# A transformer block's front on one core: unit products ahead of the first products, two chunks turned by TensorE, the first raw tile in halves, another order of loads

## Chip, cores, metric

The kernel runs on one core of a Trainium2 chip. The metric is the device time of one execution in microseconds, median of several. All values in this document are from executions of the fast state. A ratio of times is between executions of the same rounds on the same chip; the parts read from traces are compared across chips, since nearly every kernel was traced on one chip only.

## The reference

The inputs are q, k, v of 8 x 8 x 576 x 64, a norm gain, two weight matrices of 512 x 2048 and 2048 x 512, and two scalars.

```python
kv  = einsum('bhsd,bhse->bhde', k, v)
out = einsum('bhsd,bhde->bhse', q, kv)
x   = out / sqrt(mean(out*out, -1) + 1e-6) * g_norm      # -> (4608, 512)
h   = x @ w_in
y   = (s * relu(h)**2 + b) @ w_out                       # float32
```

## The kernel before

Tokens are handled in chunks of 128 rows; chunks 0 to 3 form the first block and are the only ones computed ahead of the first dense product. The weights come in as raw tiles `w_raw` of 128 x 1024 words, are converted by ScalarE (high words, low words) and put together by VectorE (a shift, an add). "Turned" means transposed; "Square" is ScalarE's pass over an attention product that begins its norm, and "root" the square root in it. The dense products ("slots", 16 records in the trace each: a float32 product makes two records, a transpose one; in after the first 18 unit products are 36 records, the four transposes of a q chunk 4) need converted weights `wa`, `wb` and the turned, normed rows `xT`. All that follows concerns the first 40 us. `x6(1)` below is the dense product whose weights are `w_t`; b_ps is the small product that spreads the bias.

```python
def kv_product(b):
    for i in range(2):                      # the two halves of k and v
        kv = kv_in.pop((b, i))
        ...                                 # 36 products of 64x64
    ...                                     # copies to bd_kv: ScalarE l=0, VectorE l=1

def attention(c, first=False):
    def turn():                             # q chunk -> qT
        for p in range(NP):
            nc.tensor.transpose(ps[:, p, :], q_in[c][:, p * P : p * P + P], ident)
        if first: nc.vector.tensor_copy(out=st["qT"], in_=ps)
        else:     nc.scalar.copy(st["qT"], ps)
    def product():                          # 16 products of 32 rows, then the sum of squares
        ...
        nc.scalar.activation(st["xn"], st["x"], AF.Square)
        nc.vector.reduce_sum(st["ss"], st["xn"], axis=mybir.AxisListType.X)
    def norm(): ...                         # root on ScalarE, inverse and product on VectorE
    def turn_x():                           # VectorE turns, ScalarE scales 128x256, 4 times for 2 chunks
        nc.vector.transpose(out=to, in_=...)
        ...

# the front
load_q(0, two); send_w(); load_q(2)
for _ in range(2): send_w()
kv_product(0)
turn[0](); turn[1](); product[0](); product[1](); norm[0]()
hi(0); turn[2](); norm[1](); shift(0); turn_x[0](); lo(0); plus(0)
product[2](); turn[3](); turn_x[1](); product[3]()
hi(1); norm[2](); shift(1); lo(1); plus(1); norm[3]()
slots0[0](); turn_x[2](); turn_x[3]()
for step in (hi, lo, shift, plus): step(2)
slots0[1]()
```

`hi` and `lo` are ScalarE's conversions of a raw tile, `shift` and `plus` are VectorE's two steps.

Of the kernel before, what the change touches and what calls it, by code (L numbers as in the profile page):

```python
# [8 lines left out]
FP32 = mybir.dt.float32  # L9
U32 = mybir.dt.uint32  # L10
# [5 lines left out]
def kernel(  # L16
# [96 lines left out]
    def load_q(c, queues=(nc.sync, nc.sync)):  # L113



        t = qp.tile([P, 2 * DM], FP32, name="q_sb", tag="q")
        pieces = []
        for i in range(2):
            if c + i < R:  # L120
                q_in[c + i] = t[:, i * DM : i * DM + DM]
                to = q_in[c + i].rearrange("p (h d) -> p h d", h=H)
                for s, (b, j, _) in enumerate(parts(c + i)):
                    queues[s].dma_start(
                        out=to[s * HB : s * HB + HB],
                        in_=q[b].rearrange("h (p j) d -> p j h d", j=R)[:, j],
                    )
                continue
            w = 4 * i
            for b, j, n in parts(c + i):  # L130
                if pieces and pieces[-1][1] == b and pieces[-1][2] + pieces[-1][3] == j:
                    pieces[-1][3] += n
                else:
                    pieces.append([w, b, j, n])
                w += n
            q_in[c + i] = t.rearrange("p (a w) -> p a w", a=NP)[:, :, i * P : i * P + P]
            if c + i == R:
                q_in[R] = t[:, DM:].rearrange("p (a w) -> p a w", a=NP)
        for w, b, j, n in pieces:
            src = q[b].rearrange("h (t j) d -> h t j d", j=JC)  # L140
            to = t.rearrange("p (a w d) -> p a w d", a=NP, d=32)
            if c < R:
                to, w = t[:, DM:].rearrange("p (a w d) -> p a w d", a=NP, d=32), 0
            for h in range(H):
                for a in range(2):
                    rows = slice(32 * (2 * (h % 2) + a), 32 * (2 * (h % 2) + a) + 32)
                    nc.sync.dma_start(
                        out=to[rows, h // 2, w : w + n, :],
                        in_=src[h, :, j : j + n, a * 32 : a * 32 + 32],
                    )  # L150
# [32 lines left out]



    def pairs(i):
        return w_raw[i].rearrange("p (n two) -> p n two", two=2)

    def fold_hi(i):
        if wide:  # L190
            hi = w_raw[i].bitcast(FP32).rearrange("p (n two) -> p n two", two=2)[:, :, 1]
            nc.scalar.activation(hi, hi, AF.Prelu, scale=2.0**-112, alpha=-(2.0**32))

    def round_lo(i):
        if wide:
            lo = pairs(i)[:, :, 0]
            nc.scalar.activation(lo, lo, AF.Copy, scale=2.0**-29)

    def shift_hi(i, dst):
        if wide:  # L200
            nc.vector.tensor_scalar(
                out=dst.bitcast(U32), in0=pairs(i)[:, :, 1],
                scalar1=3, scalar2=None, op0=ALU.logical_shift_left,
            )
        else:
            nc.vector.tensor_copy(out=dst, in_=w_raw[i])

    def add_lo(i, dst):
        if wide:
            d = dst.bitcast(U32)  # L210
            nc.vector.tensor_tensor(out=d, in0=d, in1=pairs(i)[:, :, 0], op=ALU.add)
        del w_raw[i]

    def add(o, a, b):
        nc.vector.tensor_tensor(out=o, in0=a, in1=b, op=ALU.add)  # L215
# [92 lines left out]
    nc.gpsimd.dma_start(out=b_col, in_=moe_b.to_broadcast((P, 1)))  # L308
    b_sq = const.tile([P, P], FP32, name="b_sq")
    nc.vector.memset(b_sq, 1.0)  # L310
    nc.vector.tensor_scalar(out=b_sq, in0=b_sq, scalar1=b_col, scalar2=None, op0=ALU.mult)
    b_row = const.tile([P, DM], FP32, name="b_row")

    def bias_row():

        ps = ps_t.tile([P, DM], FP32, name="b_ps", tag="t")
        matmul(ps, b_sq, b_row, True, True)
        nc.scalar.copy(b_row, ps)


    def kv_product(b):


        ps = [ps_t.tile([P, 2, D], FP32, name="kv_ps", tag="t") for _ in range(2)]
        for i in range(2):
            kv = kv_in.pop((b, i))
            for j in range(R):
                for l in range(2):
                    for r in range(2):
                        rows = slice(r * HB, r * HB + HB)  # L330
                        nc.tensor.matmul(  # L331
                            ps[r][l * HB : l * HB + HB, i, :],
                            lhsT=kv[rows, 0, l, j, :],
                            rhs=kv[rows, 1, l, j, :],
                            start=(j == 0),
                            stop=(j == R - 1),
                        )
        for r in range(2):
            for l in range(2):
                ls = slice(l * HB, l * HB + HB)  # L340
                to = bd_kv[b % 2][ls, 2 * r : 2 * r + 2, ls].rearrange("p i (c e) -> p i c e", c=KC)
                src = ps[r][ls].rearrange("p i (e c) -> p i c e", c=KC)
                if b == 0 and l == 1:
                    nc.vector.tensor_copy(out=to, in_=src)
                else:
                    nc.scalar.copy(to, src)
# [3 lines left out]
    def attention(c, first=False):  # L350
# [2 lines left out]



        b, b1 = parts(c)[0][0], parts(c)[-1][0]
        st = {}

        def turn():
            st["qT"] = attp.tile([P, NP, P], FP32, name="qT", tag="qT")  # L360
            if c >= R:
                nc.vector.transpose(out=st["qT"], in_=q_in[c])
                return
            if c == 0:
                ps = ps_a.tile([P, NP, P], FP32, name="qT_ps", tag="x")
            else:
                ps = ps_t.tile([P, NP, P], FP32, name="qT_ps", tag="t")
            for p in range(NP):
                nc.tensor.transpose(ps[:, p, :], q_in[c][:, p * P : p * P + P], ident)  # L369
            if first:  # L370
                nc.vector.tensor_copy(out=st["qT"], in_=ps)
            else:
                nc.scalar.copy(st["qT"], ps)

        def product():
            if first:
                ps = bank_of("att", "xy"[c % 2]).rearrange("p b (m n) -> p (b m) n", m=2)
            else:
                ps = ps_a.tile([P, NP, P], FP32, name="x_ps", tag="x")
            for w in range(4):  # L380
                for p in range(NP):
                    nc.tensor.matmul(  # L382
                        ps[32 * p : 32 * p + 32, w, :],
                        lhsT=st["qT"][:, p, 32 * w : 32 * w + 32],
                        rhs=bd_kv[(b if w < 2 else b1) % 2][:, p, :],
                        start=True,
                        stop=True,
                    )
# [21 lines left out]
        def turn_x():  # L410
            u, j = divmod(c, 4)
            if j == 0:
                xT[u] = xp.tile([P, KC, 2 * TB], FP32, name="xT", tag="xT")
            to = xT[u][:, :, j * P : j * P + P]
            nc.vector.transpose(
                out=to, in_=st["xn"].rearrange("p h d -> p (h d)").rearrange("p (c x) -> p c x", c=KC)
            )
# [4 lines left out]
                        to[:, i], to[:, i], AF.Copy, scale=g_col[:, i : i + 1]  # L422
                    )

        return turn, product, norm, turn_x

    def whole(product, norm):
        def run():
# [54 lines left out]
    def mm1_plain(s):  # L483


        def block(lower, half, name, tag):
            ps = bank_of("c", tag)
            w = (wb if lower else wa)[s]
            for b in range(2):
                for c in range(KC):  # L490
                    matmul(
                        ps[:, b, :], w[:, c, b], xT[0][:, c, half * TB : half * TB + TB],
                        b == 0 and c == 0, c == KC - 1,
                    )
# [269 lines left out]
    def place(n):  # L764
        s, lower = where(n)
        return w_in_at(s, lower) if n < 2 * NS else w_out_at(s, lower)

    def hi(n):
        fold_hi(blocks[n])

    def lo(n):
        round_lo(blocks[n])

    def shift(n):
        shift_hi(blocks[n], place(n))

    def plus(n):
        add_lo(blocks[n], place(n))
        send_w()

    def more(n):

# [9 lines left out]
        load_kv(0, i, kv0p, two, tag="kv")  # L792
    load_q(0, two)
    send_w()
    load_q(2)
    for _ in range(2):
        send_w()
    kv_product(0)
# [1 line left out]
    gp = ctx.enter_context(tc.tile_pool(name="gp", bufs=NS))  # L800


    turn, product, norm, turn_x = zip(*(attention(c, True) for c in range(4)))
    turn[0]()
    turn[1]()
    product[0]()
    product[1]()
    norm[0]()
    hi(0)
    turn[2]()  # L810
    norm[1]()
    shift(0)
    turn_x[0]()
    lo(0)
    plus(0)
    product[2]()
    turn[3]()
    turn_x[1]()
    product[3]()
    hi(1)  # L820
    norm[2]()
    shift(1)
    lo(1)
    plus(1)
    norm[3]()
    slots0 = [slot for s in range(NS) for slot in mm1_plain(s)]
    slots0[0]()
    turn_x[2]()
    turn_x[3]()
    for step in (hi, lo, shift, plus):  # L830
        step(2)
    slots0[1]()

    def side_of(u):

        if u + 1 >= U:
            return {}
        turn, product, norm, turn_x = zip(*(attention(c) for c in range(4 * u + 4, 4 * u + 8)))
        product = [whole(*steps) for steps in zip(product, norm)]
        side = {  # L840
            2: [turn[0]],
# [130 lines left out]
```

## Time and profile before

| | before |
|---|---|
| time, median of 4 | 975.06 us (974.03 to 975.20) |
| span of the profiled execution | 972.7 us |
| TensorE busy | 951.6 us, 98% |
| first slot starts | 27.92 us |
| second slot starts | 33.82 us |
| fourth slot starts | 40.80 us |
| from there to the end | 931.9 us |

The last row is the one to keep: from the fourth slot on TensorE has work all the time, so whatever the front does is seen in the start of the fourth slot, and whatever is given back later is seen in the rest. The rest is "span less start of the fourth slot" throughout.

The prediction shows the main lines. Three more of the timeline of before matter (start in us, length in us, engine, line, operation, tiles, count, and in brackets the idle time of that engine before it with what ended it). They are what VectorE and ScalarE do between the k-v product and the first attention product:

```profile
14.64 0.29 DVE L311 TENSOR_SCALAR b_sq<-b_sq,b_col 128x128 f32<-128x128 f32 x1 [13.61 <-DMA b_col<-in_moe_b_dram]
15.11 0.42 ACT L346 COPY bd_kv<-kv_ps 64x128 f32<-64x128 f32 x2 [13.10 <-PE kv_ps L331]
15.40 0.50 DVE L344 COPY bd_kv<-kv_ps 64x128 f32<-64x128 f32 x2 [0.47 <-ACT bd_kv L346]
```

VectorE stood for 13.61 us at the bias square, since it comes ahead of the copies in its order and its transfer landed at 14.6. Before the change this cost nothing: the k-v product itself ended at 15.0.

### The profile page before, as it was taken

Reading aid. Unit: us, or ns where it says so; the run is one execution under the profiler, and the core shown is the slowest. Engines: PE = TensorE matmul, PEld = TensorE weight load, DVE = VectorE, ACT = ScalarE, POOL = GpSimd, SP = SyncE. Lnnn points to the kernel's source line nnn. Section 1 sums busy time; section 2 is a strip of 40 time slices with the busy share of each in tenths; the row PEclk is TensorE's granted clock in tenths of the full one; section 3 lists DMA queues with packets and bytes.
Section 4 is the critical chain, followed back from the end, with each engine's and each line's share of the span. In section 5 each row is a group of like instructions: output and inputs, shape, how many; then the busy total and the mean of one; then the engine's idle time right before and its main releaser. Section 6 shows DMA issues by size and latency. Waiting matters only on the chain.

```text
span 972.7 us, 15160 instructions
## 1 busy us (share of the span) xinstructions
PE 951.6 (98%) x6406; PEld 824.5 (85%) x6406; DVE 490.1 (50%) x804; ACT 193.4 (20%) x359; POOL 6.7 (1%) x18
## 2 busy tenths in 40 slices
PE   4899999999999999999999999999999999999997
PEld 4788888888888888888888888888888888888886
DVE  2789667454445534554346344644455345544431
ACT  2674132101220112111210212011201111111100
POOL 2000000000000000000000000000000000000000
PEclk9999999999999999999999999999999999999999
DMA  9688828622553346142363256225213440422032
GB/s 237 195 288 254 260 77 213 156 98 97 138 112 111 118 141 136 55 150 67 102 138 147 68 136 154 88 90 149 65 44 130 128 89 16 152 64 117 1 130 86
DMA packets 106931, 121.59 MB, mean 125 GB/s; under 512 B 74352, under 2 KB 80752, under 8 KB 99568
## 3 DMA queue, kind: packets, MB, share of 16 engines
q1 hardware_dynamic: 104816, 119.12, 41.8%
q10 hardware_dynamic: 1728, 1.51, 0.6%
q8 instruction: 50, 0.82, 0.4%
q14 instruction: 17, 0.14, 0.0%
q0 software_dynamic: 320, 0.00, 0.0%
HBM read 103.81 MB, written 16.78 MB: 124 GB/s over the span
## 4 chain that ended last, share of the span: by engine, by line
PE 95%; DMA 2%; DVE 1%; ACT 1%; SPq 0%; issue 0%; ACTq 0%; DVEq 0%
PE x_ps L87 50%; PE y_ps L87 31%; PE z_ps L87 9%; PE x_ps L382 3%; PE kv_ps L331 2%; DMA kv_sb<-in_v_dram 1%; DMA w_sb<-w 1%; PE qT_ps L369 0%; DVE xn L401 0%; ACT xT L421 0%; DVE ss L393 0%; SPq L99 0%; SPq L609 0%; ACT xn L391 0%; DVE o L590 0%
## 5 line engine op out<-in xcount | busy, mean ns | idle before, releaser
L87 PE MATMUL x_ps<-w_sb,a 128*128 128x256 f32 x768 | 172.4, 381 | 0.0
L87 PEld LDWEIGHTS x_ps<-w_sb,a 128*128 128x128 f32 x768 | 144.8, 190 | 21.9 <-issue 2.8
L87 PE MATMUL y_ps<-w_sb,a 128*128 128x256 f32 x640 | 142.9, 380 | 1.3 <-DMA w_sb<-w 1.3
L87 PEld LDWEIGHTS y_ps<-w_sb,a 128*128 128x128 f32 x640 | 120.9, 190 | 19.1 <-DMA w_sb<-w 1.7
L87 PE MATMUL x_ps<-xs,ws 128*128 128x256 f32 x512 | 121.0, 379 | 0.0
L87 PE MATMUL y_ps<-xs,wb 128*128 128x256 f32 x512 | 121.0, 379 | 0.0
L517 ACT COPY r<-x_ps 128x512 f32<-128x512 f32 x96 | 56.3, 586 | 295.7 <-PE x_ps L87 289.0
L87 PEld LDWEIGHTS x_ps<-xs,ws 128*128 128x128 f32 x512 | 97.3, 190 | 13.2
L87 PEld LDWEIGHTS y_ps<-xs,wb 128*128 128x128 f32 x512 | 97.3, 190 | 13.2
L215 DVE TENSOR_TENSOR a<-y_ps,r 128x512 f32<-128x512 f32 x64 | 44.0, 687 | 122.2 <-ACT r L517 122.2
L87 PE MATMUL x_ps<-xT,wa 128*128 128x256 f32 x384 | 91.2, 385 | 0.1
L87 PEld LDWEIGHTS x_ps<-xT,wa 128*128 128x128 f32 x384 | 74.0, 193 | 10.7 <-ACT xT L421 0.3
L474 DVE SCALAR_TENSOR_TENSOR a<-a 128x512 f32<-128x512 f32 x96 | 66.4, 692 | 3.3
L590 DVE SCALAR_TENSOR_TENSOR or<-x_ps,s_col,b_row 128x256 f32<-128x256 f32 x52 | 25.0, 482 | 76.1 <-PE x_ps L87 72.9
L87 PE MATMUL x_ps<-xT,ws 128*128 128x256 f32 x256 | 61.1, 381 | 0.0
L87 PE MATMUL z_ps<-xT,wa 128*128 128x256 f32 x256 | 60.5, 379 | 0.0
L550 DVE TENSOR_TENSOR a<-a 128x512 f32<-128x512 f32 x32 | 22.1, 692 | 76.0 <-ACT a L549 76.0
L391 ACT ACTIVATE xn<-x_ps 128x512 f32<-128x512 f32 x34 | 20.3, 597 | 192.9 <-PE x_ps L382 190.9
L87 PE MATMUL x_ps<-w_sb,s 128*128 128x256 f32 x256 | 57.3, 382 | 0.0
L87 PEld LDWEIGHTS x_ps<-w_sb,s 128*128 128x128 f32 x256 | 48.1, 190 | 7.6 <-issue 1.4
L87 PEld LDWEIGHTS z_ps<-xT,wa 128*128 128x128 f32 x256 | 48.6, 190 | 6.6
L87 PEld LDWEIGHTS x_ps<-xT,ws 128*128 128x128 f32 x256 | 48.1, 190 | 6.7
(94 smaller groups left out, 803.6 us busy)
## 6 DMA issues: line engine op xcount, KB each, us to landing
w_sb<-w SPq DMA_DIRECT2D x56, 1024.0 KB, 5.2
kv_sb<-in_k_dram SPq DMA_DIRECT2D x30, 288.0 KB, 4.8
kv_sb<-in_v_dram SPq DMA_DIRECT2D x30, 288.0 KB, 6.2
w_raw<-in_moe_w_in_dram SPq DMA_DIRECT2D x8, 1024.0 KB, 6.9
w_raw<-in_moe_w_out_dram SPq DMA_DIRECT2D x8, 1024.0 KB, 5.3
out_dram<-o SPq DMA_DIRECT2D x104, 64.0 KB, 1.7
q_sb<-in_q_dram SPq DMA_DIRECT2D x144, 32.0 KB, 2.1
w<-w_up SPq DMA_DIRECT2D x3, 1024.0 KB, 8.2
```

The costliest lines, as they stand in the source:

```text
L87: nc.tensor.matmul(o, lhsT=lhsT, rhs=rhs, start=start, stop=stop, skip_group_check=True)
L215: nc.vector.tensor_tensor(out=o, in0=a, in1=b, op=ALU.add)
L331: nc.tensor.matmul(ps[r][l * HB : l * HB + HB, i, :], lhsT=kv[rows, 0, l, j, :], rhs=kv[rows, 1, l, j, :], start=(j == 0), stop=(j == R - 1),)
L382: nc.tensor.matmul(ps[32 * p : 32 * p + 32, w, :], lhsT=st["qT"][:, p, 32 * w : 32 * w + 32], rhs=bd_kv[(b if w < 2 else b1) % 2][:, p, :] ...
L391: nc.scalar.activation(st["xn"], st["x"], AF.Square)
L474: nc.vector.scalar_tensor_tensor(t, t, 0.0, t, ALU.max, ALU.mult)
L517: nc.scalar.copy(st[name], src)
L550: nc.vector.tensor_mul(t, t, t)
L590: nc.vector.scalar_tensor_tensor(o, ps, s_col, other, ALU.mult, ALU.add)
```

## The change

The intent is to shorten the front. Products of the unit matrix fill TensorE's waits, so that its clock is up when the k-v products come (the author's estimate then; the second half of k-v took 1.50 us in after, 2.59 in before); chunks 0 and 1 are multiplied undivided and turned by TensorE instead of VectorE; the first raw tile is converted in two halves, so that work for the chunks comes in between; the bias square moves to where it is used; two of the four later q pieces go to ScalarE's queue. Cut to its core:

```diff
-    load_q(2)
+    load_q(2, two[::-1])
-    nc.vector.tensor_scalar(out=b_sq, ...)           # at the start
     def bias_row():
+        nc.vector.tensor_scalar(out=b_sq, ...)       # where it is used
+    def warm(n):
+        for _ in range(n):
+            matmul(ps[:, 0, :P], ident, ident, True, True)
     def kv_product(b):
         for i in range(2):
+            if b == 0:
+                warm((18, 7)[i])
     def product():
-            for w in range(4): ...                   # 16 products of 32 rows
+            if c < 2:
+                for p in range(NP):
+                    matmul(ps[:, p, :], st["qT"][:, p, :], bd_kv[0][:, p, :], True, True)
+            for w in range(4 if c >= 2 else 0): ...
     def turn_x():
+            if c < 2:
+                ...                                  # 4 transposes on TensorE
+                for i in range(KC):                  # 4 scaled copies of 128x128 on ScalarE
+                    nc.scalar.activation(to[:, i], ps[:, i], AF.Copy, scale=g_col[:, i : i + 1])
+                return
-    norm[0](); hi(0); turn[2](); norm[1](); shift(0); turn_x[0](); lo(0); plus(0) ...
+    warm(7)
+    norm[0](); hi(0, 0); norm[1](); shift(0, 0); hi(0, 1); lo(0, 0); plus(0, 0)
+    turn_x[0](); turn_x[1](); turn[2](); turn[3](); lo(0, 1); take[2](); take[3]()
+    shift(0, 1); product[2](); plus(0, 1); hi(1); product[3]() ...
```

The diff has more that this cut leaves out and that no run undoes by itself: the copy of chunk 1's qT goes to ScalarE, beside VectorE's of chunk 0; a slot goes through the four parts of its input dimension with both weight halves inside each; the roots of chunks 2 and 3 stand behind the second raw tile's conversions; and the second slot stands ahead of the third tile's.

In TensorE records: 32 unit products add 64, two products of 8 instead of 32 records take 48 away, 8 transposes come in, so 24 more.

> **What bounds the kernel now.** I read the page first. Its first table gives TensorE 98% of the span:
>
> ```profile
> PE 951.6 (98%) x6406; PEld 824.5 (85%) x6406; DVE 490.1 (50%) x804; ACT 193.4 (20%) x359; POOL 6.7 (1%) x18
> PE   4899999999999999999999999999999999999997
> ```
>
> Only the first of the 40 slices (24.3 us each) is not full, and the change touches only that one. So the next view is the timeline of the first 40 us, where each line has start, length, engine, tile and count:
>
> ```profile
> 12.43 2.59 PE L331 MATMUL kv_ps<-kv_sb 64*64 64x64 f32 x72 [1.42 <-DMA kv_sb<-in_v_dram]
> 14.96 1.97 PE L369 MATMUL qT_ps<-ident,q_sb 128*128 128x128 f32 x8
> 18.66 0.60 ACT L391 ACTIVATE xn<-x_ps 128x512 f32<-128x512 f32 x1 [3.12 <-PE x_ps L382]
> 20.21 1.13 ACT L192 ACTIVATE w_raw<-w_raw 128x1024 f32<-128x1024 f32 x1
> 26.76 1.08 PE L382 MATMUL y_ps<-bd_kv,qT 128*32 128x128 f32 x32 [2.69 <-DVE qT L371]
> 27.92 5.41 PE L87 MATMUL x_ps<-xT,wa 128*128 128x256 f32 x16
> 32.45 1.23 DVE L211 CUSTOM_DVE_ANT_0 wb<-w_raw,wb 128x2048 uint16<-128x2048 uint16 x1
> 33.82 3.69 PE L87 MATMUL y_ps<-xT,wb 128*128 128x256 f32 x16 [0.49 <-DVE inv L399]
> 37.35 3.62 PE L87 MATMUL x_ps<-xT,wa 128*128 128x256 f32 x16
> ```
>
> The last piece of v lands at 12.3. Then a latency chain runs: k-v product, turned q, product, norm, turned x. The first dense slot (x_ps, 16 records) starts at 27.92, the second (y_ps) at 33.82, when the second weight tile wb is finished (32.45 + 1.23). From there slots follow every 3.45 us, and the waits of TensorE from 34 to 200 us sum to 0.5 us. So **the front is worth what it moves the start of the second slot**, 33.82, provided that nothing later takes it back.
>
> Two more readings. The granted clock, in stretches of 1 us, is halved near 29 to 31:
>
> ```profile
> 28.00:29.00 1.00, 1.00 (x4) 0.81 (x5) 0.00 (x0) 1.00 (x4) 0.00 (x0) 0.70 0.90 285
> 29.00:30.00 1.00, 1.00 (x4) 0.82 (x3) 0.42 (x1) 1.00 (x3) 0.00 (x0) 0.50 1.04 393
> 30.00:31.00 1.00, 1.00 (x3) 0.79 (x3) 0.47 (x2) 1.00 (x3) 0.00 (x0) 0.50 0.51 197
> 31.00:32.00 1.00, 1.00 (x4) 0.80 (x3) 0.98 (x2) 0.96 (x2) 0.00 (x0) 0.59 0.06 25
> ```
>
> (The clock is the third column from the end.) This is why the first slot takes 5.41 where the others start 3.45 apart. And VectorE shows no idle time in the timeline from 61.86 to 101.5, ending with
>
> ```profile
> 60.72 1.23 DVE L211 CUSTOM_DVE_ANT_0 w_up<-w_raw,w_up 128x2048 uint16<-128x2048 uint16 x1 [0.35 <-ACT w_raw L197]
> 99.03 2.49 DVE L218 TENSOR_TENSOR w_t<-w_dn,w_up 128x512 f32<-128x512 f32 x4
> 102.96 1.02 PE L87 MATMUL b_ps<-b_row,b_sq 128*128 128x512 f32 x2
> ```
>
> [...] 72 k-v products take 2.59 us at 12.43 (36 ns each), the same products 17 ns each at 110.82 (144 in 2.42); the granted-clock column says 1.00 for both, so it isn't right before its first event. [...] The trace shows the 16 engines full from 3 to 18 us. [...] the four 128-element copies at 113.33 took 1.09, so 272 each. I use that.
>
> **The change, part by part.**
>
> *Unit products.* 18 (36 records[...]) start when the unit matrix exists, about 1.4 us, and end between 7 and 8.8; k and v of the first half arrive at 8.8. They and the 7 between the halves delay nothing, and the clock should be up. The second half then takes 72 x 17 ns = 1.2 rather than 2.59: it ends at 13.65, not 15.02. The eight q transposes need 105 ns each (0.42 of loads for four at 20.28) rather than about 200, but wait for the last q piece, 14.2.
>
> *Bias square.* VectorE waited 13.6 us for b_col until 14.64; moving this away is needed, else it would now hold the k-v copies.
>
> *Two qT copies side by side, undivided products.* ScalarE copies at 13.75; VectorE's copies end near 14.55, qT of chunk 0 at 15.2. The product is 8 records of 108 ns: Square of chunk 0 starts near 16.2 rather than 18.66. **Gain so far 2.4 us.** The sum of squares ends at 17.5, the first root at 17.8.
>
> *First raw tile.* Here I expect a new wait. The first half's conversion stands on ScalarE behind the first root and ahead of the second root, and needs the whole tile. The tile was issued at 10.36 and took 9.1 us: it landed at 19.46. Before, ScalarE reached it at 20.21, so that cost nothing. Now ScalarE comes at 17.8. Two of the four later q pieces now go on the ACT ring, beside this tile rather than behind it: 256 KB at about 300 GB/s, up to 0.9 us. I choose L = 20.1 for the landing.
>
> *From L on*, ScalarE in order: half 0.55, root 0.3, half 0.55, low half 0.55, eight scaled 128-element copies 8 x 0.27 = 2.2, low half 0.55, Square 0.6, second tile 1.1, Square 0.6, its low words 1.1: 8.1 us, to L + 8.1. VectorE's shift (0.65) ends about then and its add (1.25) ends at **L + 9.35 = 29.45**. TensorE turns x at L + 1.8, turns q of chunks 2 and 3, does both products by L + 5.2, and starts the first slot there: four of its eight products need only the first half of wa. With 3.45 us it ends at L + 8.65, so the second slot waits for wb and starts at 29.5. **Gain 33.82 - 29.5 = 4.3.**
>
> *Given back later.* Raw tile 5 is sent when tile 2 is converted. That now stands behind both first relu copies (2 x 0.6) on ScalarE: scaling ends at 34.2 (38.13 before), relus 35.3, both conversions 37.5, add 38.8 (41.49 before): gain 2.7, not 4.3. Tiles 5 to 8 wait for their transfers in the profile before (at 47.44, 50.71, 54.03, 58.5), so VectorE's full stretch begins only about 2.5 earlier and ends at 101.5 - 2.5 = 99.0. The moved bias square (0.29) stands at its very end, and b_ps needs it. Before, TensorE reached b_ps at 102.75, 1.0 after VectorE would have had it (101.5 + 0.29). So TensorE's gain is cut to about 2.5 + 1.0 = **3.5 us**, a stall of 0.8 at b_ps.
>
> *Clock.* Between the 7 products after the second attention product (end 18.3) and the second x transposes (21.9), TensorE does only half a microsecond of transposes[...]. Before, a busier stretch (24.1 to 28.2, one product of 1.08) was followed by half clock. If this happens here, transposes and products double until about 28.2: second slot near 31.0, tile 2 at 40.1, so a gain of 1.4 + 1.0 = 2.4 at b_ps. I give it one half.
>
> **The rivals.** (a) *All is kept*: no bias stall, clock up: 4.3, 970.8. For it: the 1.0 us slack is an estimate. Against: VectorE has no idle time in that stretch. (b) *The load takes it all*: L at 21.5 or later[...]; every microsecond of L is one of the gain: 2.1 or less, 973.0. For it: engines full to 18; against: from 18 to 20 they are only half busy, so there is room. (c) *Cold clock*: 972.7. (d) *ScalarE is the bound*: 8.1 of the 9.35 us after L are its own; copies of 350 ns would add 0.6.
>
> **Range and chances.** Between 971.6 (warm) and 972.7 (cold), with some weight on an earlier landing: 975.1 - 3.2 = 971.9. L by +-0.8, the clock and the bias stall make 970.2 to 973.7. A change of 2% is 19.5 us; the whole time before the second slot is 33.8 and 12.3 of it is transfer, so neither side is plausible: 0.01 each.
>
> **What would show it.** Right: 72 k-v products of the second half in about 1.2 us; ScalarE idle for over 1.5 us ahead of the first conversion, released by the raw tile's transfer; second slot at 29 to 31.5; TensorE idle up to 1 us at b_ps behind b_sq. Wrong: ScalarE not waiting there (the tile landed by 18), a second slot before 28.5 or after 32.5, idle TensorE after 110 us that was not there before, or k-v products still at 36 ns each.

Beside it: the forecast came to 975.1 - 3.2 = 971.9 us, from a gain of 3.5 with the clock up and 2.4 at half clock. Cut out of it, marked, is what no trace or run of this case shows: four statements ahead of the parts, a remark in "Clock", the reason in rival (b), and the pace of a unit product, so that the end "between 7 and 8.8" is left as an estimate without its ground (in after the 36 records ran from 1.35 to 7.37). No number of the sum from L on is cut. That the unit products would bring the clock up was the author's estimate, beside the 36 and 17 ns a record in the trace of before, whose record of the granted clock begins only at 18.17 us. Estimates from the same trace are the 300 GB/s (it moved 279 from 3 to 18 us), the 108 ns (half of the 216 of a 128x256 record, 3.45 us for 16; the eight records took 0.97 in after, 121 each) and the steps from L on (conversion 1.13, root 0.29, Square 0.60, shift 0.69, add 1.23).

## The result and the profile after

| | before | after |
|---|---|---|
| time, median of 4 | 975.06 us | 972.73 us (971.14 to 973.44) |
| span of the profiled execution | 972.7 us | 970.5 us |
| second slot | 33.82 us | 31.13 us |
| fourth slot | 40.80 us | 38.51 us |
| rest | 931.9 us | 932.0 us |

The ratio is 0.9976, with a 95% interval of 0.9959 to 0.9993. Ratios here are the mean time of one kernel's fast runs over that of the other's of the same rounds, so not quite the ratio of the medians. The change is within 2%, and faster by about 2.3 us.

On the page of after, TensorE has its 24 records more, and is busy longer although the span is shorter: unit products are busy time that does no work.

```profile
PE 958.3 (99%) x6430; PEld 832.7 (86%) x6430; DVE 488.7 (50%) x803; ACT 194.6 (20%) x366; POOL 6.7 (1%) x18
```

The timeline of after, the lines that answer to those of before:

```profile
12.69 1.50 PE L350 MATMUL kv_ps<-kv_sb 64*64 64x64 f32 x72 [0.73 <-DMA kv_sb<-in_v_dram]
17.10 0.60 ACT L421 ACTIVATE xn<-x_ps 128x512 f32<-128x512 f32 x1 [0.91 <-PE x_ps L87]
...
19.99 0.67 ACT L201 ACTIVATE w_raw<-w_raw 128x512 f32<-128x512 f32 x1 [1.21 <-DMA w_raw<-in_moe_w_in_dram]
...
24.69 1.45 PE L412 MATMUL x_ps<-bd_kv,qT 128*32 128x128 f32 x32
...
29.85 1.23 DVE L221 CUSTOM_DVE_ANT_0 wb<-w_raw,wb 128x2048 uint16<-128x2048 uint16 x1
...
31.13 3.72 PE L87 MATMUL y_ps<-xT,wb 128*128 128x256 f32 x16 [0.46 <-DVE wb L221]
...
34.95 3.72 PE L87 MATMUL x_ps<-xT,wa 128*128 128x256 f32 x16
```

Read it in order. The second half of k-v took 1.50 us instead of 2.59. The first Square starts at 17.10 instead of 18.66. Then comes the new wait: ScalarE stood 1.21 us until 19.99 for the transfer of the first raw tile, where before it came at 20.21 and found the tile there (issued at 10.36 and 9.1 us under way, it had landed at 19.46). So 1.56 us of gain in hand became 0.22. What follows the landing is shorter: 11.1 us to the second slot, against 13.6 in before. The two parts, 0.22 and 2.5, are the gain of 2.69. The third slot loses 0.3 of it again (34.95 against 37.35), since it waited 0.50 us for ScalarE's scaling of xT of chunks 2 and 3; at the fourth slot 2.29 us are left.

The stretches of 1 us of after, where the column after POOL's is the granted clock, show where half clock came in, between the unit products and the first dense slot:

```profile
22.00:23.00 1.00, 0.98 (x5) 1.00 (x6) 0.85 (x2) 0.96 (x4) 0.00 (x0) 0.55 0.98 367
23.00:24.00 1.00, 1.00 (x7) 1.00 (x6) 0.10 (x2) 0.91 (x4) 0.00 (x0) 0.50 1.05 383
```

The product of chunk 2 therefore took 1.45 us, against 1.08 at full clock.

At b_ps, where the prediction expected some gain to be given back, the timeline of after shows no wait:

```profile
100.10 0.28 DVE L326 TENSOR_SCALAR b_sq<-b_sq,b_col 128x128 f32<-128x128 f32 x1
100.45 0.41 PEld L87 LDWEIGHTS b_ps<-b_row,b_sq 128*128 128x128 f32 x2
```

The bias square ended at 100.38 and TensorE loaded it at 100.45: 0.07 us to spare.

### The profile page after: what moved, and what is told of

It reads as the page before. It is cut to its first block, busy times and chain, and to the rows that moved or that the text cites. A ratio compares the mean times of both kernels' runs of the same rounds, so it can differ in the third digit from the quotient of the medians.

```text
span 970.5 us, 15215 instructions
## 1 busy us (share of the span) xinstructions
PE 958.3 (99%) x6430; PEld 832.7 (86%) x6430; DVE 488.7 (50%) x803; ACT 194.6 (20%) x366; POOL 6.7 (1%) x18
## 4 chain that ended last, share of the span: by engine, by line
PE 95%; DMA 2%; DVE 1%; ACT 1%; SPq 0%; issue 0%; ACTq 0%; DVEq 0%
PE x_ps L87 50%; PE y_ps L87 31%; PE z_ps L87 9%; PE x_ps L412 3%; PE kv_ps L350 2%; DMA w_raw<-in_moe_w_in_dram 1%; DMA kv_sb<-in_k_dram 1%; DMA w_sb<-w 1%; PE qT_ps L391 0%; DVE xn L431 0%; DVE xT L455 0%; ACT xT L461 0%; ACT w_raw L206 0%; SPq L649 0%; DVE o L630 0%
```

## The experiments

My theory: the landing of the first raw tile, L, sets the end of the front; everything won ahead of it is lost, and what counts is the work between L and the second slot, and the clock in it. The rivals: the clock alone gives the gain; the order of loads gives it; or the turning by TensorE does.

Twelve runs were made, four per chip, with 5 rounds. The first table has what the profiled execution of each shows. "From L" is the time from the start of the first conversion to the second slot; "wait" is how long ScalarE stood for the tile ahead of it.

| kernel | time, median us | ratio to before, 95% | wait | L | second slot | from L | clock in the stretch | fourth slot | rest |
|---|---|---|---|---|---|---|---|---|---|
| before | 975.06 | 1 | none | 20.21 | 33.82 | 13.6 | partly half | 40.80 | 931.9 |
| after | 972.73 | 0.9976 (0.9959 to 0.9993) | 1.21 | 19.99 | 31.13 | 11.1 | half | 38.51 | 932.0 |
| a0_again | 971.80 | 0.9972 (0.9959 to 0.9984) | 1.86 | 21.02 | 31.98 | 11.0 | half | 39.35 | 932.0 |
| a1_fill | 973.14 | 0.9983 (0.9970 to 0.9995) | 1.21 | 19.91 | 29.85 | 9.9 | full | 37.23 | 934.0 |
| a2_nowarm | 973.01 | 0.9986 (0.9973 to 0.9998) | none | 20.56 | 32.02 | 11.5 | half | 39.31 | 933.4 |
| a3_oldbias | 972.09 | 0.9977 (0.9964 to 0.9991) | 0.41 | 20.65 | 30.61 | 10.0 | full | 37.99 | 932.0 |
| b1_same | 972.08 | 0.9966 (0.9952 to 0.9979) | 1.39 | 20.03 | 29.97 | 9.9 | full | 37.35 | 931.9 |
| b2_pad | 974.53 | 0.9987 (0.9975 to 1.0000) | 2.08 | 20.59 | 31.71 | 11.1 | half | 39.09 | 933.1 |
| b3_split | 972.38 | 0.9969 (0.9957 to 0.9982) | none | 20.06 | 30.99 | 10.9 | full | 38.37 | 932.0 |
| b4_best | 971.65 | 0.9968 (0.9954 to 0.9982) | none | 20.21 | 29.82 | 9.6 | full | 37.20 | 932.0 |
| c1_whole | 973.42 | 0.9974 (0.9959 to 0.9990) | 1.74 | 20.98 | 31.98 | 11.0 | full | 39.36 | 932.2 |
| c2_dveturn | 976.27 | 1.0005 (0.9990 to 1.0020) | 2.57 | 21.30 | 33.37 | 12.1 | half, twice as long | 40.67 | 933.9 |
| c3_loads | 972.75 | 0.9970 (0.9952 to 0.9987) | 1.38 | 20.22 | 31.48 | 11.3 | half | 38.86 | 932.1 |
| c4_unitonly | 978.60 | 1.0033 (1.0015 to 1.0051) | none | 20.40 | 34.01 | 13.6 | partly half | 40.99 | 935.3 |

Executions of one kernel differ by 1.4 to 5.0 us (a1_fill: 972.40 to 973.77; after: 971.14 to 973.44; c4_unitonly: 976.87 to 981.89), and each run has one trace. So the medians alone tell little apart; the parts are read from the traces, each by its own L and clock. In the seven traces that have the change's order of work after L and in which ScalarE waited for the tile, "from L" is 9.9 to 10.0 at full clock (a1_fill, a3_oldbias, b1_same) and 11.0 to 11.3 at half clock (after, a0_again, b2_pad, c3_loads). This number is steady enough for a part undone to show in it. It holds only where ScalarE waited: in a2_nowarm and b3_split, with nearly the same order, ScalarE came after the tile and the norms of chunks 0 and 1 came right behind, and it is 11.5 (half clock) and 10.9 (full).

### The change again

a0_again is the changed kernel, unaltered, on another chip.

> The changed kernel unaltered, as the control of this chip for the three that follow. Expected: 972 to 973 us, second slot (first y_ps product of 16 records) at about 31.1 us, half clock from about 22 to 25.4 us, ScalarE's first conversion waiting about 1.2 us for the first raw tile, b_ps at 100.7. If its single runs scatter by 2 us again (971.1 to 973.4), then the half-clock stretch may be there in some runs and not in others.

L was 1.0 later (21.02) and the second slot 0.85 later. The time from L was 11.0, and the gain against before of that chip 0.28%.

### Unit products between the turned chunks

```diff
-    warm(7)
+    warm(11)                # ahead of the first norm
     norm[1]() ... turn_x[0]()
+    warm(4)                 # between the two turned chunks
```

> Unit products also where TensorE still waits: 11 rather than 7 after the second attention product, and 4 between the two turned chunks. Theory (the cold clock is what cost 1 to 1.5 us of the predicted gain): clock 1.00 from 22 to 26 us, products of chunk 2 near 23.8 rather than 24.69, ScalarE no longer waiting 1.5 us for it, second slot at 29.8 rather than 31.13, time about 1.3 us under the changed kernel. Rival (ScalarE's conversions after the landing are the bound, the half clock lies beside them): clock 1.00 as well, but second slot within 0.4 us of 31.1 and the time unchanged.

Clock up, and the second slot came 1.28 earlier than in after, at nearly the same L:

```profile
29.85 3.72 PE L87 MATMUL y_ps<-xT,wb 128*128 128x256 f32 x16 [0.45 <-DVE wb L221]
```

But the time was no better. The rest was 934.0, and the missing 2.1 us stand in one place of the timeline of a1_fill:

```profile
107.25 2.35 PE L350 MATMUL kv_ps<-kv_sb 64*64 64x64 f32 x144
109.53 2.43 PE L87 MATMUL x_ps<-w_t,a 128*128 128x256 f32 x10
114.04 1.45 PE L87 MATMUL x_ps<-w_t,a 128*128 128x256 f32 x6 [2.08 <-issue]
```

TensorE stops in the middle of one accumulation, with all its inputs there, for nothing that the profile knows ("issue"). Two theories were open: it comes from being 1.3 us earlier, or from the 16 records more. b1_same and b2_pad tell these apart.

### No unit products

```diff
-                warm((18, 7)[i])
-    warm(7)
```

> All unit products taken away, everything else as in the changed kernel. Theory (the landing of the first raw tile at about 20 us hides most of what the unit products save): 72 k-v products of the second half back to 2.6 us instead of 1.5, first Square at about 18.3 to 18.8 instead of 17.1, but ScalarE then waits less than 0.5 us for the tile, and the second slot moves by less than 0.8 us (to at most 31.9). Rival (the unit products are the change's gain): the second slot moves by 1.2 us or more and over half of the gain over the kernel before is gone.

The first Square came at 18.98, ScalarE reached the tile at 20.56 without a wait, and the second slot was at 32.02: 0.9 later than in after (a little past the "at most 31.9" expected), and no later than in a0_again. So without unit products the front has no wait for the tile and with them it has one; they are worth under a microsecond here. The rest was 1.4 us longer. 1.1 of it is the wait that the prediction had expected of the change itself:

```profile
102.72 1.13 PE L87 MATMUL b_ps<-b_row,b_sq 128*128 128x512 f32 x2 [1.09 <-DVE b_sq L326]
```

In this execution ScalarE stood 1.89 us for a raw tile at 62.8, and VectorE's stretch ended late: its last additions to w_t began at 99.98, in after at 97.69.

### The bias square where it was

```diff
     nc.vector.memset(b_sq, 1.0)
+    nc.vector.tensor_scalar(out=b_sq, ...)
     def bias_row():
-        nc.vector.tensor_scalar(out=b_sq, ...)
```

> The square of the bias multiplied at its old place, first on VectorE, where it waits for b_col (landing about 15.9 in the trace of the changed kernel). Theory: VectorE's k-v copies start about 16.1 instead of 14.56, the first Square is 1.6 us later (18.7), but the first conversion only 0.4 later (20.35), as the tile's landing takes over; second slot about 0.5 later, at 31.6. Rival (the front is one chain of latencies and every microsecond of it counts): second slot 1.6 later, at 32.7.

```profile
15.70 0.29 DVE L322 TENSOR_SCALAR b_sq<-b_sq,b_col 128x128 f32<-128x128 f32 x1 [14.66 <-DMA b_col<-in_moe_b_dram]
...
20.65 0.67 ACT L201 ACTIVATE w_raw<-w_raw 128x512 f32<-128x512 f32 x1 [0.41 <-DMA w_raw<-in_moe_w_in_dram]
```

VectorE held up the k-v copies, and the first Square was at 18.55, 1.45 later than in after. Yet ScalarE still waited 0.41 us for the tile. So a delay of 1.45 us ahead of L was absorbed whole in this execution: **all of it was slack**, because the tile landed late. The slack is the wait and no more: with the tile at 19.99 as in after, where ScalarE waited 1.21, some 0.25 of the delay would have shown (20.65 - 0.41 = 20.24). The clock stayed up here, so the second slot, 30.61, was even earlier than in after, and not at the 31.6 expected. The prediction's sentence that moving the bias square "is needed" holds for the order of instructions, not for the time.

### As many unit products, placed otherwise; and more of them, at the old place

b1_same has 14, 3, 11 and 4 of them (32, as in the change), b2_pad 22, 11 and 7 (40, as in a1_fill, but none between the turned chunks).

```diff
-                warm((18, 7)[i])            # the change
+                warm((14, 3)[i])            # b1_same, with warm(11) and warm(4)
+                warm((22, 11)[i])           # b2_pad, with warm(7)
```

> The filled kernel with as many unit products in all as the changed kernel (14, 3, 11 and 4 rather than 18, 7, 11 and 4, so 32 as before and not 40). In the filled kernel the second slot came at 29.85 as expected, but the gain was gone again in a stall of 2.1 us of TensorE at 111.96 that no semaphore explains, beside a read of 16 KB of instructions at 111.9. Theory (32 more TensorE instructions ahead move the border between two pieces of its instruction stream to where the transfers are full, so the next piece comes late): second slot again near 29.9, no such stall, the rest of the span from the fourth slot on 932.0 us as in the changed kernel (934.0 in the filled one), time about 970.6, 1.2 to 2 us under the filled kernel. Rival (TensorE came too early for something that shifts with it, such as the transfer or a bank): the stall is there again wherever the second slot is at 29.9, time 972.5 to 973.

> The changed kernel with eight more unit products at its very start (22 and 11 rather than 18 and 7), where TensorE waits for k and v anyway: nothing in the front moves but the number of TensorE instructions, which is that of the filled kernel. Theory of the instruction stream: fourth slot as in the changed kernel (38.5 to 39.4), a stall of 1 to 2.5 us without a semaphore near 113 and a rest of 933 to 934.5 us from the fourth slot on; time 973 to 974.5. Rival (the stall comes from being early): no stall, rest 932.0, time 971.8 to 972.7.

```profile
29.97 3.72 PE L87 MATMUL y_ps<-xT,wb 128*128 128x256 f32 x16 [0.45 <-DVE wb L221]
```

b1_same: full clock, second slot at 29.97, no stall, rest 931.9, although it is as early as a1_fill. Its median, 972.08, is not the 970.6 expected. b2_pad: half clock, as late as after and later, and the stall is there:

```profile
111.39 2.43 PE L87 MATMUL x_ps<-w_t,a 128*128 128x256 f32 x10
114.86 1.46 PE L87 MATMUL x_ps<-w_t,a 128*128 128x256 f32 x6 [1.05 <-issue]
```

In time, b2_pad is 2.4 us slower than b1_same of the same rounds (974.53 against 972.08). So the stall comes with the number of records, not with being early: it comes after the same 10 records of the same accumulation. That is what these two runs show; pieces of the instruction stream that move stay the author's theory.

### The first raw tile in two transfers

b1_same with the first raw tile sent as two halves, one on each queue.

```diff
-            nc.sync.dma_start(out=dst..., in_=src...)
+            for cs, queue in (((slice(0, KH), nc.sync), (slice(KH, KC), nc.scalar)) if i == 0 else ((slice(0, KC), nc.sync),)):
+                queue.dma_start(out=dst...[:, cs], in_=src...[:, cs, ...])
```

> The kernel of b1 with the first raw tile loaded as two halves, the one on the SP ring, the other on the ACT ring. Theory (the landing of this tile bounds the front): the first half lands at about 18.5 to 19, ScalarE's first conversion starts at 18.8 to 19.2 instead of 19.9 to 21.0, the second slot about 0.5 to 1.0 earlier than in b1. Rival (the x chain of chunk 1 or the second weight tile bounds): first conversion earlier, second slot within 0.3 us of that of b1.

ScalarE did not wait for the tile, but it came later itself, at 20.06, so nothing was won:

```profile
9.64 2.19 PE L353 MATMUL kv_ps<-kv_sb 64*64 64x64 f32 x70 [1.82 <-DMA kv_sb<-in_v_dram]
13.35 2.20 PE L353 MATMUL kv_ps<-kv_sb 64*64 64x64 f32 x72
```

In this execution the first half of v landed 0.7 later than in after, the 14 unit products had ended by then, and both halves of k-v ran at 31 ns a record (2.19 us for 70, 2.20 for 72), where after had 18 and 21. The transfers themselves did what was expected: the half that the first conversion needs landed at 18.21 (issued at 10.71, 7.5 us), the other at 19.94; in b4_best at 16.82 and 19.39. ScalarE came for it only at 20.06. Whether this helps where ScalarE comes early stays open.

### All that looked useful

b4_best has 16, 5 and 11 unit products (32), the split tile, the second root ahead of the first conversion, and the bias square on ScalarE.

```diff
+        nc.scalar.activation(b_sq, b_sq, AF.Copy, scale=b_col)
-    hi(0, 0); norm[1]()
+    norm[1](); hi(0, 0)
```

> An attempt at a version that beats both: 32 unit products (16, 5, 11), the root of chunk 1 ahead of the first conversion, the first tile in two halves on two rings, the square of the bias on ScalarE. Expected: both turned chunks done by 21.7, second slot near 28.8 to 29.3, no stall at b_ps, time 969.5 to 970.5 if no new stall of the instruction stream comes up; with one, 971.5 to 972.5.

The second slot was the earliest of all, 29.82, ScalarE did not wait for the tile (20.21), and the median was 971.65. Both miss what was expected (a second slot at 28.8 to 29.3, a time of 969.5 to 970.5), without a stall at record 852. In time it is not to be told from b1_same of the same rounds (0.9968 against 0.9966): no version is shown to beat the change.

### One part undone: the halves, the turning, the loads

```diff
-    hi(0, 0); norm[1](); shift(0, 0); hi(0, 1); lo(0, 0); plus(0, 0) ... lo(0, 1) ... shift(0, 1) ... plus(0, 1)
+    hi(0); norm[1](); shift(0); lo(0); plus(0)               # c1_whole

-            if c < 2:                                        # in product and in turn_x
+            if False:                                        # c2_dveturn; and range(4) for all chunks

-    load_q(2, two[::-1])
+    load_q(2)                                                # c3_loads
```

> The changed kernel with its first raw tile converted whole, in the old order: one conversion of 1.1 us, then the second root, one shift, one low half, one add; the halves are the only thing undone. My theory: after the tile has landed (L, the start of the conversion that waited for it) ScalarE's order of work sets the start of the second slot, and the whole conversion holds the second root back by 0.55 us, the low half of 1.1 stands ahead of the scaled copies, but no half is left between the copies and the second tile. In the changed kernel and in the equal run the second slot came 11.1 and 11.0 us after L with half clock, 9.9 with the clock up (in the kernels with unit products between the turned chunks). I expect L + 10.5 to L + 11 with the clock up, or L + 11.5 to 12.5 at half clock. Rival: the halves are worth nothing, since the second tile's conversions end the chain in both: within 0.3 of the same figures. Time = fourth slot + 932: about 1 us later than the changed kernel at the same L and clock.

> The changed kernel with chunks 0 and 1 turned as chunks 2 and 3 are: products of 32 rows (32 records each) and VectorE's transposes with two 256-element scalings on ScalarE; only the turning by TensorE is undone. My theory: VectorE has room between the two norms, a transpose of 128x512 is one instruction of about 0.6 us a chunk, and ScalarE's scaling becomes 4 copies instead of 8, so the second slot comes within 0.7 us of L + 11.1 (half clock) or L + 9.9. Rival: turning by TensorE is what gains most, because VectorE, which transposes, shifts and adds, becomes the bound: over 1.5 us later. If TensorE has more records in front (about 48 more for two products, minus 8 transposes), a stall for nothing that the profile shows, as the kernels with 40 unit products had at the 110 us mark, may come back: rest of 933 instead of 932.

> The changed kernel with the later q pieces all on SP's queue, as before the change: only the order of loads is undone. My theory: the two pieces on the ACT queue travel beside the first raw tile and delay it a little, so without them L is earlier: 19.4 to 19.7 instead of 19.9 to 20.0 in the first run (21.0 in the equal one, on another chip), and the second slot is up to 0.5 us earlier, as long as q of chunks 2 and 3 arrives by 20.5; at half clock 30.6 to 31.2. Rival: the order of loads is what lets chunks 2 and 3 be early; with it undone q of chunk 3 lands after 22 and the second slot is 1 us later or more. Rest 932 either way.

**Halves** (c1_whole): 11.0 us from L at full clock, where the change has 9.9 to 10.0. So the halves are worth about 1.05 us after L, as my theory had it; the rival (nothing) falls. The clock stayed up here without further unit products: 1.00 in each microsecond from 20 to 26, with TensorE busy for 2.2 of the six. In after it fell to 0.50 at 22.09, with TensorE busy for 1.15 of the three from 19 to 22. The record of the granted clock begins at 18.17 in before and changes at 28.41 and 31.82; in after it begins at 5.03 and changes at 22.09 and 25.51: in both at whole multiples of 3.41 us from its beginning, which differs. So chance may decide which side a gap falls on (an estimate from these two traces); the runs do not let one foretell the clock of such a gap. Both traces of the change itself fell to half clock.

```profile
20.98 1.11 ACT L201 ACTIVATE w_raw<-w_raw 128x1024 f32<-128x1024 f32 x1 [1.74 <-DMA w_raw<-in_moe_w_in_dram]
...
31.98 3.72 PE L87 MATMUL y_ps<-xT,wb 128*128 128x256 f32 x16 [0.43 <-DVE wb L221]
```

**Turning** (c2_dveturn, which also undoes the undivided products): 12.1 from L at half clock, against 11.0 to 11.3. But this is no clean 0.8 to 1.1, since its half clock lasted 6.83 us (23.07 to 29.89) instead of 3.41, and both products of chunks 2 and 3 fell into it:

```profile
26.19 1.94 PE L412 MATMUL x_ps<-bd_kv,qT 128*32 128x128 f32 x32 [1.09 <-DVE qT L398]
...
27.90 1.93 PE L412 MATMUL y_ps<-bd_kv,qT 128*32 128x128 f32 x32
```

In after they took 1.45 and 1.05. The product of chunk 2 began 4.89 after L, behind VectorE's transposes and copies, against 4.70 in after (half clock) and 3.89 in a1_fill (full clock). So up to there the turning is worth 0.2 at half clock and, as an estimate from these numbers, 1.0 at full clock; a comparison at like clocks was not run, and theory (within 0.7) and rival (over 1.5) stay undecided. The kernel stalls too, for 1.24 us.

```profile
110.69 2.19 PE L350 MATMUL kv_ps<-kv_sb 64*64 64x64 f32 x131
114.13 0.45 PE L350 MATMUL kv_ps<-kv_sb 64*64 64x64 f32 x13 [1.24 <-issue]
```

**Loads** (c3_loads): 11.3 from L at half clock and L = 20.22, inside what the two executions of the change show (19.99 and 21.02), with the later q in time. The second slot shows no effect of the order of loads, and an L of 19.4 to 19.7, as I expected, did not come. The tile's time from issue to landing says more: 9.0 to 9.6 us in the three traces with the later q on SP's queue (before 9.1, c3_loads 9.6, c4_unitonly 9.0), and 9.3 to 10.8 in the nine with two pieces on ScalarE's and the tile whole; on this chip 9.6 and 9.0 against 10.7 and 10.8 (c1_whole, c2_dveturn). That points to my theory, but the ranges overlap, and the next two raw tiles start earlier too in the nine (about 14 to 15 us instead of 16.2 to 16.6), which no run separates.

### One part alone: the unit products

c4_unitonly is the kernel before, with `warm(18)` and `warm(7)` in the first k-v product and nothing else: 50 records more.

> The kernel before with one part alone: the 18 and 7 unit products ahead of the halves of the first k-v product, and nothing else. My theory: k-v of the second half falls from 2.59 to about 1.5 us and would be done near 14.1, but VectorE still stands in the bias square until 14.6 to 14.9, and the conversion of the first raw tile could start no earlier than its landing (19.5 to 20): so the second slot is within 0.5 of 33.8 unless the clock itself changes the later products (the kernel before ran its product of chunk 1 and first slot partly at half clock). Rival: the clock was the main thing; with it up from the start the second slot comes 1.5 us earlier or more, nearly the whole gain of the change. Rest 932, or 933 if 50 more records bring the stall at 110 us.

```profile
16.02 0.28 DVE L311 TENSOR_SCALAR b_sq<-b_sq,b_col 128x128 f32<-128x128 f32 x1 [14.99 <-DMA b_col<-in_moe_b_dram]
...
34.01 3.69 PE L87 MATMUL y_ps<-xT,wb 128*128 128x256 f32 x16 [0.70 <-DVE inv L407]
```

The k-v product's second half fell to 1.69 us and gained nothing: VectorE stood at the bias square, whose transfer landed at 16.0 here. The second slot came at 34.01 (33.82 in before). The rival, that the unit products alone give the gain, falls: with this bias square ahead they could give nothing, and without it at most the 0.7 between the tile's landing (19.73) and ScalarE's arrival (20.40). And TensorE stalled for 1.98 us, and its clock fell again behind it (the mean granted from the start is 0.99 at 114.5 us and 0.97 at 131); with it the kernel is slower than before, by 3.5 us.

### The stall: where it stands

The four kernels that stall stop at different places: after 10 records of x6(1) (a1_fill, b2_pad), at the end of the k-v product (c4_unitonly), inside it (c2_dveturn). What they share is the number of TensorE records done by then. Each line is the sum over one stretch, from the start of a kernel's execution to a time within its stall; the number behind the second value is the count of TensorE's records.

The stretch of a1_fill:

```profile
0.00:113.00 113.00, 107.78 (x852) 94.58 (x853) 78.27 (x120) 54.80 (x81) 6.68 (x18) 1.00 0.87 264
```

That of b2_pad:

```profile
0.00:114.00 114.00, 108.65 (x852) 95.44 (x853) 78.39 (x120) 54.65 (x81) 6.67 (x18) 0.99 0.86 262
```

That of c2_dveturn:

```profile
0.00:113.90 113.90, 104.72 (x853) 91.43 (x854) 79.49 (x122) 53.26 (x73) 6.67 (x18) 0.97 0.85 253
```

That of c4_unitonly:

```profile
0.00:114.50 114.50, 102.89 (x852) 89.72 (x853) 79.50 (x121) 53.33 (x74) 6.67 (x18) 0.99 0.85 259
```

852, 852, 853, 852, in kernels whose work differs by then. So TensorE stopped at a fixed place of its instruction stream. The author's theory is a read of instructions that came late. The table of queues on the page of after has such reads:

```profile
q8 instruction: 50, 0.82, 0.4%
```

50 reads of 16 KB. That they are TensorE's is not shown; its 6,430 records make 129 a read (an estimate from the page). In the trace of after the reads of 32.80, 60.56 and 86.35 us come with 336, 463 and 582 records begun, 127 and 119 apart. At that distance the next would be due at about 705 (an estimate; over the whole trace the distance varies, from 18 to 256). It came at 113.48, with 838 records begun, while the 16 DMA engines were full (queue 1 alone took 100.7% of their time from 113 to 114). In the theory it is the k-v product that eats the distance: 144 records in 2.35 us, 61 a microsecond, where dense slots take 4.6. In a1_fill, 842 records were done at the end of the k-v product (109.5), and the ten that were left lasted 2.4 us; the read came at 111.84 and the next record ran at 114.04. In after 826 were done at its end (110.8), and 26 were left, about 5.3 us of work (16 of x6(1) in 3.55, four transposes in 0.44, six of the next slot in 1.3).

Shown: the stall comes at record 852 in four kernels with 40 to 64 records more than before (c4_unitonly 50, a1_fill and b2_pad 40, c2_dveturn 64), and in none of the traces with 24 more or fewer. Also shown: in all four the next record starts 1.24 to 1.41 us after that read has landed (a1_fill 1.27, b2_pad 1.41, c2_dveturn 1.35, c4_unitonly 1.24), while in the eight traces with 24 records more the 853rd starts later than that by itself: 1.68 in after, 1.69 to 1.80 in a0_again, c1_whole and c3_loads, over 3 in the others. So the change runs about 0.3 to 0.4 us clear of the stall, as an estimate from these numbers, if its border lies at the same record. Argued, not shown: that the late read itself is the cause. No run moved the read alone.

## Why the prediction was right, point by point

The time (971.9 predicted, 972.73 and 971.80 measured on two chips) and the verdict were right; so was the main mechanism. By its own steps:

- **Unit products, clock.** Right in kind: the k-v half ran at 18 to 21 ns a record instead of 36. The size was 1.50, not 1.2.
- **First Square at 16.2, a gain of 2.4.** Mis-sized: it was 17.10, a gain of 1.56. Of the missing 0.9, 0.54 is the k-v product, which ended at 14.19 instead of 13.65 (it began 0.26 later and took 0.3 longer); the rest lies in the copies that follow it. It cost nothing, since ScalarE still waited 1.21 for the tile; in a3_oldbias, with a later tile, 1.45 more was absorbed.
- **ScalarE waits for the first raw tile.** Right in kind: 1.21 us in after, 1.86 in a0_again. In after it was half of what the steps gave (17.8 to 20.1, so 2.3; "over 1.5" as the sign), because ScalarE was late itself. L was 19.99, predicted 20.1. The reason given for L, that the q pieces on ScalarE's queue delay the tile, is supported in part by the times from issue to landing under c3_loads, and not shown.
- **From L to the second slot, 9.35 at full clock.** It was 9.9 to 10.0: 0.6 more. The copies took 0.27 each at full clock (0.30 in after), so rival (d), which needed 350 ns, did not come true; its 0.6 is met by accident. In a1_fill ScalarE was done at L + 8.26, close to the predicted 8.1, but VectorE's add began only at L + 8.66: its shift was said to end at about 8.1 and ended at 8.52, since VectorE did the sum of squares of chunk 3 (27.15 to 27.84) ahead of it.
- **The clock, one half.** In both traces of the change half clock came; in the first the second slot, 31.13, lay 0.1 from the 31.0 of that branch. Both branches are real: a1_fill, b1_same and a3_oldbias show the other.
- **Given back at b_ps.** In the half-clock branch VectorE was to gain 1.4 there, and TensorE at most 1.0 more. It was 1.34 for VectorE (w_t at 97.69 instead of 99.03) and 2.29 for TensorE, with 0.07 us to spare, so the slack of 1.0 was sized right. That the total agrees so well with the 2.4 of this branch is in part luck: the prediction took its 0.4 off at b_ps, while in the trace the gain fell from 2.69 to 2.29 between the second and the fourth slot, and b_ps took nothing. The stall of 0.8 belonged to the full-clock branch, and there the step failed: VectorE was said to end at 99.0 + 0.29, but in a1_fill and b1_same the bias square ended at 98.54 and 97.59, 0.6 and 1.7 us ahead of its load at 99.17 and 99.29. VectorE's gain was sized too small: its additions to w_t began at 95.85 and 94.90 instead of 99.03, so 3.2 and 4.1 where 2.5 was predicted. It differs by execution: in a2_nowarm a raw tile came late, and the stall was there, with 1.09.
- **What was not foreseen.** The third slot's wait of 0.5 for scaled xT, and the stall at record 852, which came in the four kernels with 40 to 64 records more than before; no trace with the change's 24 has it.

Where the gain is, then: 1.05 us from the halves at full clock (one trace), 0.2 to an estimated 1.0 from the turning, depending on the clock, both after L; the unit products under 1 by themselves. These are not to be added up, as each depends on the clock in its trace, which alone makes 1.0 to 1.3 of difference. Left open: what the parts that no run undid are worth (the slot's inner order, the order of roots and slots); the scatter of 1 us and more either way among executions of one kernel, part of which is the landing L (19.9 to 21.0 in the traces of the change's order of work in which ScalarE waited), and whether stalls at record 852 come in some executions of the change that were not traced.

## What to carry to other kernels

Ahead of shortening a chain, look for what lands on it from outside: here what was won before the raw tile's landing became a wait of 1.2 us, and only work after it counted; the slack ends where the wait ends. Read a front by its waits and by one number that lies behind it (span less the start of the first slot from which TensorE is never idle), because times of 1 us difference drown in the scatter. Filler instructions were not free here even where the engine was idle: with 16 records more than the change in the front TensorE stopped a hundred microseconds later, for 1.05 us in b2_pad and 2.08 in a1_fill.
